# Batches 2 and 3 of the attention in plain fp32 on halves of the array, and the second layer's weights decoded beside it

## The chip, the core and the metric

The kernel runs on one core of a Trainium2 chip. The metric is the device time of one execution in microseconds (us). The engines are TensorE (PE, with its weight loads as PEld), VectorE (DVE), ScalarE (ACT) and GpSimd (POOL); SyncE (SP) issues nearly all of the DMAs. SBUF is the on-chip memory, PSUM the eight banks that TensorE writes.

## The reference

Attention over 4 batches, 8 heads, 576 positions and 64 columns, with a retrieved memory mixed in, and behind it two matrix products with a gated activation between them, all in fp32:

```python
scores = scale * q @ k.T          # causal mask, softmax -> a
local = a @ v
q_p = where(q > 0, q, exp(q) - 1) + 1
mem_out = (q_p @ M_prev) / (q_p . z_prev + 1e-6)
x = g * mem_out + (1 - g) * local  # g = sigmoid(beta), one per head; x is 2304 x 512
h = x @ w_in                       # w_in 512 x 2048, given as 8-byte floats
out = (h * sigmoid(1.702 * h)) @ w_out   # w_out 2048 x 512, given as 8-byte floats
```

## The kernel before

**Stages.** The work is planned in slots. `first_queries` (0 to 46 us) does the first 256 queries of batch 0 and decodes the first of the sixteen blocks of `w_in`. Then sixteen pairs of heads (four batches, four pairs each) run through `plan_prep` and `plan_attend`: pair p starts at slot `K0[p]`, batch 0 at slots 0, 7, 14, 21, the others 8 slots apart from 29 on, so batch 1 has slots 29 to 61 and batches 2 and 3 slots 61 to 133. `step()` emits what is planned for a slot, and then fills TensorE with matmuls of the first layer (`first_moe`) up to a budget per slot (`PACE`, 2.2 us at first, 2.7 us from slot 60). It charges each matmul a modelled time (`mm`). The first layer takes 8 chunks of tokens (256 to 320 wide) times 16 blocks times 12 matmuls, 1536 in all. After the last pair, a tail emits the rest of them (390 to 463 us). Then the second layer runs (463 to 653 us), a product of 2 by 2 blocks in seven partial products: `units` of 12 matmuls each, 84 units.

**Attention, two ways.** `plain = b < MP` with `MP = 2`: batches 0 and 1 multiply in plain fp32 with both heads side by side on halves of the array (`s_both`: 64 rows for each head; `pv_both`: 64 columns for each head). Their matmuls are issued in unbroken groups (`group`), which wait once for all that they need. Batches 2 and 3 multiply in fp32r: operands are split into a high part and a rest. `split_hi` (ACT), `split_lo_k`, `split_lo_q`, `vlo` (POOL) split keys, queries and values; `stack_hi` and `stack_lo` copy them by DMA into the tiles `W0` and `W1`; `s_unit` and `pv_unit` multiply; `ev_unit` splits each piece of the transposed weights (ACT copy, DVE subtraction); `xsum` adds the two halves of the result. One fp32 matmul stands in the trace as two records.

**The first layer's results.** `gate` copies each block from PSUM into a tile `hk` (three buffers), on ACT or, for every second block, on DVE while `len(moe_ps) == 1`, which is until the tail; then SP stores it to DRAM (`gd`, line 856). Blocks go to the two banks `ps_m`; in the tail, from the 21st block on (`LATE = 20`), to the six banks `ps_w`.

**The second layer's weights.** `conv_pair(kk)` runs in the tail for kk = 0 to 7, two in five steps. For both halves it loads 512 KB of raw `w_out` on POOL's queue (line 983), scales it into a bank of `ps_w` (`scale`, ACT, line 987), and puts the bits together (`bits`, three DVE instructions, lines 992, 993, 995). Then `sums` makes the four sums that the seven products need (DVE), `w_hi` copies them to fp32r (ACT), and `w_lo` subtracts (DVE), giving the tile `wo{kk}`. For kk = 0 to 4 (`EARLY`) that is done in the tail, for 5 to 7 behind it. The unit n needs the tiles 2p and 2p+1, where p = n mod 4.

**The seam.** `split(n)` makes the operands of unit n (`oh` on ACT, `ol` on DVE) from a tile of `gd` that `load_g` (line 1030) brought back and `gelu` (ACT, line 1034) passed through. The first two units' operands are loaded early. The other tiles of the second layer lie over the first layer's: in the list of pools behind `left.close()`, `reuse_waits="tile"` makes each wait only for the tiles that lay under it.

Tile schedules the program: the order on each engine and queue comes from priorities and a timeline that it keeps, not from the text alone.

The lines of the helpers: `mm` 126, `tr` 132, `copy` 137 (ACT) and 140 (DVE), `tt` 145. The max of the softmax is line 546, the exponentials 552, the scaling of rows 555, the second layer's matmul 1071.

Of the kernel before, what the change touches and what calls it, by code (L numbers as in the profile page):

```python
# [8 lines left out]
F32 = mybir.dt.float32  # L9
# [25 lines left out]
def tile_attention_memory_moe(ctx, tc, kq, vq, mem, zz, beta, w_in, w_out, out):  # L35
# [4 lines left out]
    MP = 2  # L40
# [3 lines left out]
    LATE = 20  # L44
    W0 = 6
    CONV = [-7, -6, -5, -3, -1, 1, 3, 5, 7, 9]
    PSUM = bass.MemoryType.PSUM
# [13 lines left out]
    dr = pool(ctx, "dr", space=bass.MemoryType.DRAM)  # L61
    ldp = pool(attn, "ldp", side="right")
# [335 lines left out]

    def load_vq(p):
        b, c = pairs[p]  # L400

        vr = (att.tile([128, 5, 128], F32, name="vs", bufs=2) if b < MP else ldp.tile([128, 5, 128], F32, name="vr"))
# [10 lines left out]
    def plan_prep(p):  # L413
# [3 lines left out]
        rest, plain = b < MB, b < MP  # L417
        T0 = 2 if rest else 0
        qo = 256 if rest else 0

        def split_hi():
            kqr = raws[p]["kq"]
            P["hi"] = att.tile([128, S + SQ], F32R, name="hi")
            copy("A", P["hi"][:, :S + SQ - qo], kqr[:, :S + SQ - qo])

        def split_lo_k():
            P["lok"] = att.tile([128, S], F32R, name="lok")
            sub("P", P["lok"], raws[p]["kq"][:, :S], P["hi"][:, :S])

        def split_lo_q():  # L430
            P["loq"] = att.tile([128, SQ], F32R, name="loq")
            n = SQ - qo
            sub("P", P["loq"][:, :n], raws[p]["kq"][:, S:S + n], P["hi"][:, S:S + n])

        def stack_hi():
            P["W"] = [att.tile([128, S + 1024 - 2 * qo], F32R, name=f"W{h}", bufs=2) for h in range(2)]
            for h in range(2):
                r, o = slice(64 * h, 64 * h + 64), slice(64 - 64 * h, 128 - 64 * h)
                w = f32(P["W"][h])
                n = S + 512 - qo  # L440
                nc.sync.dma_start(w[r, :n], f32(P["hi"])[r, :n])
                nc.sync.dma_start(w[o, S:n], f32(P["hi"])[r, S:n])

        def stack_lo():
            for h in range(2):
                r, o = slice(64 * h, 64 * h + 64), slice(64 - 64 * h, 128 - 64 * h)
                nc.sync.dma_start(f32(P["W"][h])[o, :S], f32(P["lok"])[r, :])
                n = 512 - qo
                for rows in (r, o):
                    nc.sync.dma_start(f32(P["W"][h])[rows, S + n:S + 2 * n], f32(P["loq"])[r, :n])  # L450

        def vhi():
            P["vs"] = att.tile([128, 5, 2, 2, D], F32R, name="vs", bufs=2)
            copy("A", P["vs"][:, :, :, 0], raws[p]["v"].rearrange("p t (h d) -> p t h d", h=2))

        def vlo():
            sub("P", P["vs"][:, :, :, 1], raws[p]["v"].rearrange("p t (h d) -> p t h d", h=2),
                P["vs"][:, :, :, 0])
# [4 lines left out]

        def msplit():
            P["ms"] = att.tile([128, 2, 2, D], F32R, name="ms", bufs=2)
            copy("A", P["ms"][:, :, 0], raws[p]["m"], gt[:, c:c + 1])
            nc.vector.scalar_tensor_tensor(
                out=P["ms"][:, :, 1], in0=raws[p]["m"], scalar=gt[:, c:c + 1], in1=f32(P["ms"][:, :, 0]),
                op0=ALU.mult, op1=ALU.subtract)
# [38 lines left out]
        def qev():  # L508
            qh, ql = P["qpt"] = [att.tile([128, S], F32R, name=f"qpt{s}", bufs=2) for s in range(2)]
            if plain:  # L510
                P["qpt"] = att.tile([128, S], F32, name="qpt0", bufs=2)
                used(P["pt"][0], copy("A", P["qpt"][:, qo:512], P["pt"][0][:, qo:]))
                used(P["pt"][1], copy("V", P["qpt"][:, 512:S], P["pt"][1][:, :64]))
                return
            for pt, a, n in ((P["pt"][0][:, qo:], qo, 512 - qo), (P["pt"][1], 512, 64)):
                copy("A", qh[:, a:a + n], pt[:, :n])
                sub("V", ql[:, a:a + n], pt[:, :n], qh[:, a:a + n])
# [7 lines left out]
        if plain:  # L525
            at(s0 + 7, 51, mplain)
        else:
            at(s0 + 6, 55, vhi)
            at(s0 + 7, 50, vlo)
            at(s0 + 7, 51, msplit)  # L530
# [26 lines left out]
    def plan_attend(p):  # L557
# [4 lines left out]
        rest, plain = b < MB, b < MP  # L562
# [18 lines left out]

        def s_unit(h, i):
            n, q0 = 128 * (i + 1), S + 128 * i - qo
            q1 = q0 + 512 - qo
            ps = U["ps", h, i] = bank("ps")
            mm(ps[:, :n], P["W"][h][:, q0:q0 + 128], P["W"][h][:, :n], True, False)
            mm(ps[:, :n], P["W"][h][:, q1:q1 + 128], P["W"][h][:, :n], False, True)
# [30 lines left out]
        def s_tail():  # L618
            U["ps"] = [bank("ps") for _ in range(2)]
            o = 512 - qo  # L620
            if plain:
                kq = raws[p]["kq"]
                for f in range(2):
                    mm(U["ps"][f][:, :CH], kq[:, S + o:S + o + 128], kq[:, CH * f:CH * f + CH], True, True)
                return
            hi, lok, loq = P["hi"], P["lok"], P["loq"]
            qh, ql = hi[:, S + o:S + o + 128], loq[:, o:o + 128]
            for k, (st, mv) in enumerate(((qh, hi), (qh, lok), (ql, hi))):
                for f in range(2):
                    mm(U["ps"][f][:, :CH], st, mv[:, CH * f:CH * f + CH], k == 0, k == 2)  # L630
# [38 lines left out]
        def ev_unit(h, j):  # L669
            n = 384 if j < 0 else (320 if j < 3 else 256)  # L670
            pt = U["pt", h, j]
            if plain:
                U["e", h, j] = att.tile([128, 384], F32, name=f"e{(j + h) % 2}", bufs=4)
                x = copy("AV"[(j + h) % 2], U["e", h, j][:, :n], pt[:, :n])
                used(pt, x)
                U["ev", h, j] = x.ins.name
                return
            e = U["e", h, j] = [att.tile([128, 384], F32R, name=f"e{s}", bufs=4) for s in range(2)]
            copy("A", e[0][:, :n], pt[:, :n])
            sub("V", e[1][:, :n], pt[:, :n], e[0][:, :n])  # L680

        def pv_unit(h, j):
            ch = 0 if j < 0 else 1
            q0, n = (0, 256) if ch == 0 else (256, 320)
            first, last = j <= 0, j < 0 or j == 3
            if first:
                U["po", h, ch] = ps_o.tile([128, 512], F32, name="po")
            po, e, vs = U["po", h, ch], U["e", h, j], P.get("vs")
            ops = []

            def put(o, kt, x, y):
                for s in range(2):
                    ops.append((o, vs[:, kt, h].rearrange("p s d -> p (s d)"), e[s][:, x:y]))

            if first:
                for s in range(2):
                    ops.append((po[:, :n], P["ms"][:, h].rearrange("p s d -> p (s d)"), P["qpt"][s][:, q0:q0 + n]))
            if j < 0:
                put(po[:, :256], 0, 0, 256)
                put(po[:, 128:256], 1, 256, 384)  # L700
            elif j < 3:
                put(po[:, :320], j, 0, 320)
            else:
                put(po[:, :192], 3, 0, 192)
                put(po[:, 128:192], 4, 192, 256)
            for k, (o, l, r) in enumerate(ops):
                mm(o, l, r, first and k == 0, last and k == len(ops) - 1)
# [27 lines left out]

        def xsum(h, ch):
            r, o = slice(64 * h, 64 * h + 64), slice(64 - 64 * h, 128 - 64 * h)
            q0, n = (0, 256) if ch == 0 else (256, 320)
            if "xf" not in P:
                P["xf"] = wkp.tile([128, S], F32, name="xf")  # L740
# [58 lines left out]
        if plain:  # L799
            steps = ((3, 1), (2, 5)) if rest else ((3, 1), (2, 4), (1, 5), (0, 5))  # L800
            for i, idx in steps:
                if i:
                    at(k0 + idx, 20, lambda i=i: scores((1, 0) if i == 1 else (i,)))
# [404 lines left out]
```

## Time and profile before

| | us |
|---|---|
| median of 3 runs (650.18, 654.70, 655.16) | 654.7 |
| the profiled execution | 654.82 |
| its span, first to last instruction | 653.0 |
| around the span | 1.8 |

The span falls into the start (0 to 38 us), batch 0 (to 109 us), batch 1 (to 188 us), batches 2 and 3 (to 390 us), the tail of the first layer (to 463 us), the seam (to 480 us) and the second layer (to 653 us). The mean granted clock of TensorE is 0.988 of full speed. Matmuls are pipelined: a record's length is longer than the distance to the next one, so a cost is read from start to start. A line of the trace can be that of a helper, so groups are told apart by tiles: `ps` are scores, `pt` transposes, `po` weighted values, `pm` the first layer, `acc` the second.

### The profile page before, as it was taken

The page shows a single profiled execution, that of the slowest core. Times are in us where ns is not written, and L with a number is a line of the kernel's source. Part 1 is how long each engine was busy: PE and PEld are TensorE (multiplying, and loading weights), DVE is VectorE, ACT ScalarE, POOL GpSimd, SP SyncE. Part 2 cuts the span into 40 slices and gives each one's busy share as a digit, 9 for nine tenths or more (in the row PEclk, how much of TensorE's full clock was granted, in tenths as well). Part 3 has the DMA queues.
Part 4 walks back from the last instruction along what each step waited for, and adds up shares of the span by engine and source line. Part 5 has one row for each costly group of instructions (what it writes and reads, how often), then busy time and mean ns, then how long its engine had stood idle before and what let it go on. Part 6 is the DMA issues. An engine that isn't in the chain of part 4 may idle for free.

```text
span 653.0 us, 12028 instructions
## 1 busy us (share of the span) xinstructions
PE 600.2 (92%) x4016; PEld 547.7 (84%) x4016; DVE 454.0 (70%) x1097; ACT 399.7 (61%) x919; POOL 218.1 (33%) x276
## 2 busy tenths in 40 slices
PE   3779799999988999998999997899799999999996
PEld 2548665688757899998999997899699999999996
DVE  4889776645676577757577635986897579559943
ACT  4767556535575777668576545565886764775451
POOL 3647545533469666457574320310000000000000
PEclk9989999999999999999999999999989999999999
DMA  7948753314529866785671136765835640771002
GB/s 244 314 134 258 214 162 131 108 50 157 158 78 226 222 186 169 213 218 167 198 201 66 47 112 231 231 195 185 263 131 159 177 148 1 217 210 57 26 0 74
DMA packets 65647, 103.47 MB, mean 158 GB/s; under 512 B 6960, under 2 KB 49456, under 8 KB 65584
## 3 DMA queue, kind: packets, MB, share of 16 engines
q1 hardware_dynamic: 63280, 94.30, 48.1%
q0 software_dynamic: 2304, 8.39, 4.2%
q8 instruction: 32, 0.52, 0.4%
q14 instruction: 31, 0.25, 0.1%
HBM read 62.87 MB, written 26.69 MB: 137 GB/s over the span
## 4 chain that ended last, share of the span: by engine, by line
PE 65%; DMA 14%; DVE 8%; ACT 7%; issue 4%; SPq 1%; POOL 1%; DVEq 0%; ACTq 0%; POOLq 0%
PE acc L1071 26%; PE pm L126 18%; PE po L126 7%; PE pt L132 6%; PE ps L126 6%; DMA gd<-hk 5%; DMA xl<-xd 4%; DMA xd<-xf 2%; ACT a L552 2%; DVE ps L546 1%; DMA g<-gd 1%; DMA fq<-in_vq_dram 1%; ACT oh L137 1%; ACT hk L137 1%; ACT xh L137 1%
## 5 line engine op out<-in xcount | busy, mean ns | idle before, releaser
L126 PE MATMUL pm<-xh,wi 128*128 128x288 f32 (+2 forms) x1024 | 217.6, 302 | 14.2 <-ACT hk L137 8.1
L126 PEld LDWEIGHTS pm<-xh,wi 128*128 128x128 f32 x1024 | 165.9, 190 | 19.6 <-ACT hk L137 10.1
L1071 PE MATMUL acc<-oh,wo 128*128 128x384 f32 x672 | 160.1, 340 | 4.7 <-ACT oh L137 4.5
L126 PE MATMUL pm<-xl,wi 128*128 128x288 f32 (+2 forms) x512 | 152.0, 299 | 0.2 <-DVE xl L145 0.2
L1071 PEld LDWEIGHTS acc<-oh,wo 128*128 128x128 f32 x672 | 121.5, 190 | 6.6 <-ACT oh L137 6.3
L145 DVE TENSOR_TENSOR ol<-g,oh 128x768 fp32r<-128x768 f32 x84 | 79.3, 954 | 49.8 <-ACT oh L137 48.5
L1071 PE MATMUL acc<-ol,wo 128*128 128x384 f32 x336 | 99.4, 338 | 0.0
L126 PEld LDWEIGHTS pm<-xl,wi 128*128 128x128 f32 x512 | 96.6, 189 | 1.7 <-DVE sm L612 1.1
L137 ACT ACTIVATE oh<-g 128x768 fp32r<-128x768 f32 x84 | 70.5, 841 | 44.2 <-PE acc L1071 43.8
L555 POOL TENSOR_SCALAR a<-a,sm,g 128x512 f32<-128x512 f32 (+3 forms) x112 | 71.7, 651 | 73.0 <-DVE sm L612 60.3
L552 ACT ACTIVATE a<-ps,nm 128x512 f32<-128x512 f32 (+3 forms) x112 | 60.2, 542 | 47.0 <-DVE nm L546 46.0
L546 DVE CUSTOM_DVE_ANT_0 ps<-ps,mask 128x256 f32<-128x256 f32 (+4 forms) x144 | 68.5, 499 | 26.9 <-PE ps L126 22.8
L1071 PEld LDWEIGHTS acc<-ol,wo 128*128 128x128 f32 x336 | 62.6, 189 | 0.0
L137 ACT ACTIVATE e<-pt 128x320 fp32r<-128x320 f32 (+4 forms) x116 | 47.4, 436 | 22.6 <-PE pt L132 12.0
L126 PE MATMUL po<-e,vs 128*64 128x320 f32 (+6 forms) x416 | 58.2, 321 | 2.9 <-ACT e L137 2.9
L137 ACT ACTIVATE hk<-pm 128x288 f32<-128x288 f32 (+2 forms) x84 | 33.5, 406 | 40.8 <-DMA gd<-hk 19.1
L126 PEld LDWEIGHTS po<-e,vs 128*128 128x128 f32 (+1 forms) x416 | 46.6, 165 | 13.1 <-ACT e L137 3.6
L132 PE MATMUL pt<-ident,a 128*128 128x128 f32 x296 | 54.9, 273 | 0.0
L145 DVE TENSOR_TENSOR e<-pt,e 128x320 fp32r<-128x320 f32 (+1 forms) x80 | 37.2, 485 | 25.2 <-ACT e L137 24.0
L1034 ACT ACTIVATE g<-g 128x768 f32<-128x768 f32 x48 | 40.2, 842 | 13.8 <-DMA g<-gd 12.5
L145 DVE TENSOR_TENSOR g<-g,g 128x768 f32<-128x768 f32 x48 | 44.1, 950 | 0.2
L132 PE MATMUL pt<-ident,at 128*128 128x128 f32 x160 | 41.1, 281 | 3.4 <-ACT a L552 2.3
(144 smaller groups left out, 916.8 us busy)
## 6 DMA issues: line engine op xcount, KB each, us to landing
g<-gd SPq DMA_DIRECT2D x48, 384.0 KB, 3.8
gd<-hk SPq DMA_DIRECT2D x96, 144.0 KB, 3.1
wraw<-in_w_in_dram SPq DMA_DIRECT2D x16, 512.0 KB, 4.8
wraw<-in_w_out_dram POOLq DMA_DIRECT2D x16, 512.0 KB, 4.5
kqr<-in_kq_dram SPq DMA_DIRECT2D x8, 608.0 KB, 5.2
W<-hi SPq DMA_DIRECT2D x16, 272.0 KB, 4.0
W<-loq SPq DMA_DIRECT2D x32, 128.0 KB, 3.7
qr<-in_vq_dram SPq DMA_DIRECT2D x12, 320.0 KB, 3.1
```

The lines of the kernel that those rows point to most:

```text
L126: x = nc.tensor.matmul(out, l, r, start=start, stop=stop)
L132: nc.tensor.transpose(out, in_, idn)
L137: return nc.scalar.activation(out=dst, in_=src, func=AF.Copy, **kw)
L145: (nc.vector if eng == "V" else nc.gpsimd).tensor_tensor(out=dst, in0=a, in1=b, op=op)
L546: nc.vector.tensor_tensor_reduce(out=ps, in0=ps, in1=mk, op0=ALU.add, op1=ALU.min, scale=-0.125, scalar=1e38 if j == 0 else nm[:, j - 1:j] ...
L552: return nc.scalar.activation(out=a, in_=ps, func=AF.Exp, scale=-1.0, bias=nm, accum_out=sm)
L555: (nc.vector if eng == "V" else nc.gpsimd).tensor_scalar(out=a, in0=a, scalar1=r, scalar2=gcol, op0=ALU.mult, op1=ALU.mult)
L1034: nc.scalar.activation(out=t, in_=t, func=AF.Gelu_apprx_sigmoid)
L1071: nc.tensor.matmul(acc[b, j][:, :QN], W[2 * p + kk][:, WPART[i], sp, 128 * j:128 * j + 128], mv[:, kk], start=first and p + kk == 0 and sp ...
```

## The change

- `plain` is gone: every batch takes the path of batches 0 and 1. With it go the splits of keys, queries and values, the tiles `hi`, `lok`, `loq`, `W0`, `W1` and the DMAs that fill them, the splits in `ev_unit` and `qev`, and `xsum`. Keys and values of all batches have two buffers (`kqf`, `vr`).
- `decode(i)` for i = 0 to 15 loads half a pair of `w_out` on SP's queue and, two slots later, scales and decodes it in place in SBUF. The slots are 27, 29, ... 41 and 62, 65, ... 83. The decoded tiles stay in two new pools of four buffers of 4 KB, `rr` (left side, behind the first layer's weights) and `rl` (right side).
- `conv_pair` keeps `sums`, `w_hi` and `w_lo` alone, for kk = 0 to 3 (`EARLY = 4`), once in six steps; `sums` of these writes into the room of the raw weights. For kk = 4 to 7 all three run behind the tail.
- `gate` copies every second block on DVE in the tail too.
- `LATE = 4`: from the 5th block of the tail on, blocks take the six banks.
- The raw blocks 7, 9, ... 15 of `w_in` are loaded into `rr` instead of the tag `W1`. The second layer's saved sums share `rl`. Behind `left.close()` there are four tiles `w2` in two places of the list.

```diff
-    MP = 2
-    LATE = 20
+    LATE = 4
+    DECODE = [27 + 2 * i for i in range(8)] + [62 + 3 * i for i in range(8)]
+    EARLY = 4
+    rl = pool(ctx, "rl", 4, side="right")
...
-        if b < MP:
-            kqr = att.tile([128, S + SQ], F32, name="kqf", tag="W0", bufs=2)
-        else:
-            kqr = ldp.tile([128, S + SQ], F32, name="kqr")
+        kqr = att.tile([128, S + SQ], F32, name="kqf", bufs=2)
...
-        if not plain:
-            at(s0 + 1, 50, split_hi)
-            at(s0 + 3, 50, split_lo_k)
-            at(s0 + 3, 51, split_lo_q)
-            at(s0 + 3, 52, stack_hi)
-            at(s0 + 4, 52, stack_lo)
...
-            copy("AV"[blk % 2 == 0 and len(moe_ps) == 1], h[:, :w], ps[:, :w])
+            copy("AV"[blk % 2 == 0], h[:, :w], ps[:, :w])
...
-        raw = (att, {"tag": "W1", "bufs": 2}) if other else (cnv, {"bufs": 2})
+        raw = (rr, {"tag": "r"}) if other else (cnv, {"bufs": 2})
...
+    rr = pool(left, "rr", 4, side="left")
...
+    def decode(i):
+        kk, h = divmod(i, 2)
+        if h == 0:
+            raw2[kk] = (rr if kk < EARLY else rl).tile([128, 2, DM], F32, name="r", tag="r")
+        raw = cnv.tile([128, DM, 2], I32, name="wraw", bufs=2)
+        r = raw2[kk][:, h]
+        ri = r.bitcast(I32)
+
+        def scale():
+            nc.scalar.activation(out=r, in_=raw[:, :, 1].bitcast(F32), func=AF.Copy, scale=2.0 ** -112)
+
+        def bits():
+            nc.vector.tensor_scalar(out=ri, in0=ri, scalar1=3, scalar2=None, op0=ALU.logical_shift_left)
+            nc.vector.scalar_tensor_tensor(
+                out=ri, in0=raw[:, :, 1], scalar=-2 ** 31, in1=ri, op0=ALU.bitwise_and, op1=ALU.bitwise_or)
+            nc.vector.scalar_tensor_tensor(
+                out=ri, in0=raw[:, :, 0], scalar=29, in1=ri, op0=ALU.logical_shift_right, op1=ALU.bitwise_or)
+
+        nc.sync.dma_start(raw.rearrange("p f w -> p (f w)"), w_out[kk + KK * h].bitcast(I32))
+        at(state["slot"] + 2, 56, scale)
+        at(state["slot"] + 2, 57, bits)
+
+    for i, slot in enumerate(DECODE):
+        at(slot, 58, lambda i=i: decode(i))
...
+    def sums(kk):
+        if kk < EARLY:
+            st = cnv.tile([128, 4, DH], F32, name="st", tag="wraw", bufs=2)
+        else:
+            st = stg.tile([128, 4, DH], F32, name="st")
...
     def conv_pair(kk):
-        box = {}
         s0 = state["slot"] + 1
...
+        at(s0, 60, lambda: sums(kk))
+        at(s0 + 1, 40, lambda: new_w(w2a, kk))
+        at(s0 + 1, 41, lambda: w_hi(kk))
+        at(s0 + 1, 42, lambda: w_lo(kk))
...
-    conv_q = list(range(KK))
+    conv_q = list(range(EARLY))
...
-        if (k % 5 in (2, 4) or fill["gen"] is None) and conv_q:
+        if (k % 6 == 3 or fill["gen"] is None) and conv_q:
...
-    w2b = [pool(ctx, f"w2_{kk}", side="left", reuse_waits="tile") for kk in range(EARLY, KK)]
+    w2b = [pool(ctx, f"w2_{kk}", side="left", reuse_waits="tile") for kk in (4, 5)]
     pools[1, 1] = pool(ctx, "g11b", 2, side="left", reuse_waits="tile")
     pools["op", 1] = pool(ctx, "opb", side="left", reuse_waits="tile")
+    w2b += [pool(ctx, f"w2_{kk}", side="left", reuse_waits="tile") for kk in (6, 7)]
     pools[0, 0] = pool(ctx, "g00", 4, side="left", reuse_waits="tile")
     for kk in range(EARLY, KK):
+        sums(kk)
         new_w(w2b[kk - EARLY], kk)
         w_hi(kk)
         w_lo(kk)
```

## Rows read from the trace of the kernel before

**Rows 1.** The page: busy time of each engine, share of the span, instructions.

```profile
PE 600.2 (92%) x4016; PEld 547.7 (84%) x4016; DVE 454.0 (70%) x1097; ACT 399.7 (61%) x919; POOL 218.1 (33%) x276
```

**Rows 2.** Busy us (instructions) by stretch: PE, PEld, DVE, ACT, POOL; then clock, DMA.

```profile
109.30:148.00 38.70, 36.51 (x250) 27.39 (x248) 22.28 (x80) 19.09 (x55) 17.23 (x20) 1.00 0.30 98
148.00:172.40 24.40, 24.40 (x178) 20.48 (x176) 12.83 (x46) 10.84 (x33) 8.41 (x11) 1.00 0.37 123
172.40:206.50 34.10, 30.46 (x217) 21.71 (x216) 22.98 (x87) 23.63 (x73) 24.81 (x30) 1.00 0.64 167
206.50:390.00 183.50, 178.19 (x1367) 174.75 (x1366) 123.54 (x396) 122.28 (x343) 99.58 (x114) 1.00 0.58 164
390.00:463.40 73.40, 65.82 (x490) 64.20 (x489) 55.81 (x100) 43.69 (x88) 9.85 (x16) 1.00 0.65 207
```

**Rows 3.** The chain that ended last, in order of time: start, us, what.

```profile
425.65 16.08 PE pm L126 x120
```

**Rows 4.** Who waited for whom, 390 to 463.4 us: total, times, longest.

```profile
ACT hk L137 <- DMA gd<-hk: 13.8, 8, 4.3
PE pm L126 <- ACT hk L137: 7.6, 7, 1.7
```

**Rows 5.** Timeline of PE, a pair of batch 1 (plain): start, us, what.

```profile
163.55 0.31 PE L126 MATMUL pm<-xl,wi 128*128 128x320 f32 x1
163.70 0.46 PE L126 MATMUL pm<-xh,wi 128*128 128x320 f32 x2
164.09 0.92 PE L126 MATMUL ps<-kqf 64*128 64x384 f32 x4
164.93 0.76 PE L126 MATMUL po<-qpt,ms 128*64 128x320 f32 x4
165.52 2.23 PE L126 MATMUL po<-e,vs 128*64 128x320 f32 x20
167.68 0.77 PE L132 MATMUL pt<-ident,qp 128*128 128x128 f32 x5
```

**Rows 6.** Timeline of PE, pairs of batches 2 and 3 (split).

```profile
242.23 0.54 PE L126 MATMUL ps<-W 128*128 128x384 f32 x2
242.60 0.42 PE L126 MATMUL pm<-xh,wi 128*128 128x288 f32 x2
...
385.79 0.45 PE L126 MATMUL po<-qpt,ms 128*128 128x320 f32 x2
386.08 1.41 PE L126 MATMUL po<-e,vs 128*128 128x320 f32 x10
```

**Rows 7.** Groups by form: busy us, mean ns; idle before, releaser.

```profile
L992 DVE TENSOR_SCALAR ws<-ws 128x512 int32<-128x512 int32 x16 | 10.9, 691 | 5.7 <-ACT ws L987 5.7
L993 DVE SCALAR_TENSOR_TENSOR ws<-wraw,ws 128x512 int32<-128x512 int32 x16 | 10.9, 687 | 0.1
L995 DVE SCALAR_TENSOR_TENSOR r<-wraw,ws 128x512 int32<-128x512 int32 x16 | 10.7, 679 | 0.1
L987 ACT ACTIVATE ws<-wraw 128x512 f32<-128x512 f32 x16 | 9.8, 627 | 0.3 <-DVE r L995 0.3
L145 POOL TENSOR_TENSOR loq<-kqr,hi 128x640 fp32r<-128x640 f32 x8 | 12.5, 1561 | 0.0
L145 DVE TENSOR_TENSOR wo<-st,wo 128x1024 fp32r<-128x1024 f32 x8 | 9.8, 1219 | 1.9 <-ACT wo L137 1.9
```

**Rows 8.** The seam: timeline of PE [idle before <- who ended it].

```profile
467.63 0.34 PE L1071 MATMUL acc<-ol,wo 128*128 128x384 f32 x1
472.43 1.65 PE L1071 MATMUL acc<-oh,wo 128*128 128x384 f32 x4 [4.46 <-ACT oh L137]
```

**Rows 9.** The seam by stretch, columns as in rows 2.

```profile
472.00:474.00 2.00, 1.57 (x5) 1.58 (x6) 1.08 (x2) 2.00 (x4) 0.00 (x0) 0.50 0.99 339
474.00:476.00 2.00, 2.00 (x8) 2.00 (x7) 1.90 (x3) 1.42 (x2) 0.00 (x0) 0.50 0.93 268
```

**Rows 10.** Tile `ms` on DVE, two SBUF inputs: ns min/median/max, first and last start.

```profile
L467 DVE SCALAR_TENSOR_TENSOR ms<-mr,gt,ms x8: 351/626/1182, 188.0 to 356.7; 128x128 fp32r<-128x128 f32 x8
```

More of the change, by code (lines that the diff above doesn't have):

```diff
@@ L416, in plan_prep @@
         P = prep[p] = {}
-        rest, plain = b < MB, b < MP
+        rest = b < MB
         T0 = 2 if rest else 0
         qo = 256 if rest else 0
[L421 to L458, printed above, removed]
         def mplain():
@@ L561, in plan_attend @@
         U = {}
-        rest, plain = b < MB, b < MP
+        rest = b < MB
         qo = 256 if rest else 0
@@ L619, in s_tail @@
             U["ps"] = [bank("ps") for _ in range(2)]
[L620 to L630, printed above, removed]
+            o, kq = S + 512 - qo, raws[p]["kq"]
+            for f in range(2):
+                mm(U["ps"][f][:, :CH], kq[:, o:o + 128], kq[:, CH * f:CH * f + CH], True, True)
         def max_tail():
@@ L671, in ev_unit @@
             pt = U["pt", h, j]
[L672 to L707, printed above, removed]
+            U["e", h, j] = att.tile([128, 384], F32, name=f"e{(j + h) % 2}", bufs=4)
+            x = copy("AV"[(j + h) % 2], U["e", h, j][:, :n], pt[:, :n])
+            used(pt, x)
+            U["ev", h, j] = x.ins.name
         def pv_both(j):
@@ L797, in flush @@
                 group(*late)
[L799 to L803, printed above, removed]
-        for i, idx in (steps if plain else ((3, 1), (2, 3), (1, 5), (0, 7))):
+        for i, idx in ((3, 1), (2, 5)) if rest else ((3, 1), (2, 4), (1, 5), (0, 5)):
+            if i:
+                at(k0 + idx, 20, lambda i=i: scores((1, 0) if i == 1 else (i,)))
+            k = k0 + idx
             for h in range(2):
-                k = k0 + idx + (h if i and not plain else 0)
-                if not plain:
-                    at(k, 10, lambda h=h, i=i: s_unit(h, i))
                 at(k + 1, 10, lambda h=h, i=i: max_unit(h, i))
@@ L813, in plan_attend @@
                 at(k + 2 + (h if i >= 2 else 0), 10, lambda h=h, i=i: scale_unit(h, i))
-        order = [(h, j) for h in range(2) for j in range(4)]
-        if plain:
-            order = [(h, j) for j in range(4) for h in range(2)]
+        order = [(h, j) for j in range(4) for h in range(2)]
         if not rest:
@@ L940, in tile_attention_memory_moe @@
     moe_ps.append((ps_w, "pm2"))
-    KK = NB // 2
-    EARLY = 5
     QN = 384
@@ L972, in conv_pair @@
     def conv_pair(kk):
-        box = {}
         s0 = state["slot"] + 1
-        def room():
-            raw2[kk] = [stg.tile([128, DM], F32, name=f"r{h}") for h in range(2)]
-            raw2[kk].append(stg.tile([128, 4, DH], F32, name="st"))
-        at(s0 + 2, 59, room)
-        def load(h):
-            box["raw", h] = (cnv, stg)[kk % 2].tile([128, DM, 2], I32, name="wraw", bufs=2)
-            nc.gpsimd.dma_start(box["raw", h].rearrange("p f w -> p (f w)"), w_out[kk + KK * h].bitcast(I32))
@@ L999, in sums @@
-        def sums():
-            ra, rb, st = raw2[kk]
-            tt("V", st[:, 0], ra[:, DH:], rb[:, DH:], ALU.add)
-            tt("V", st[:, 1], st[:, 0], ra[:, :DH], ALU.subtract)
-            tt("V", st[:, 2], ra[:, :DH], ra[:, DH:], ALU.subtract)
-            tt("V", st[:, 3], rb[:, :DH], st[:, 1], ALU.subtract)
-        for h in range(2):
-            at(s0, 5, lambda h=h: load(h))
-            at(s0 + 2, 60, lambda h=h: scale(h))
-            at(s0 + 2, 61, lambda h=h: bits(h))
-        at(s0 + 3, 60, sums)
```

84 lines of the change are left out of this document (20 added, 64 removed).

## The prediction

> **What bounds the kernel now.** I read the page first, then the busy time by stretch, then who waited in the tail, then single pairs and the seam on TensorE's timeline.
>
> TensorE is busy for 92% of the span [rows 1]. By stretch, length less busy time is what it sat idle: 2.2 us in 109 to 148, nothing in 148 to 172, 3.6 in 172 to 206, 5.3 in 206 to 390, 7.6 in the tail [rows 2]. So TensorE bounds every stage, and a change that doesn't shorten its own work can win only those idle pieces and the seam. The reader is to see that the share of the other engines (DVE 70%, POOL 33%) matters only where it makes TensorE wait.
>
> The 7.6 us of the tail have one cause. TensorE waits seven times for the copy of `hk` on ACT, 7.6 us in all, and these copies wait eight times, 13.8 us in all and 4.3 at the longest, for the store of an earlier `hk` [rows 4]: three buffers, two banks, and a DMA system at 0.65 of its time [rows 2] because sixteen raw blocks of `w_out` come in at the same time.
>
> At the seam TensorE runs two units without a pause, ends at 467.97 and starts again at 472.43, 4.46 us later, released by an `oh` on ACT [rows 8]. Behind the pause the granted clock is 0.50, the lower of its two levels (1.2 GHz), for at least 3.57 us of busy time [rows 9]; at half speed that loses 1.8. The seam costs 6.3 us.
>
> **The change, part by part**, against the profiled execution: 653.0 us of span and 1.8 around it, 654.8; the median of the runs, 654.7, is the same.
>
> 1. Plain instead of split on TensorE. Read from start to start: the larger part of the weighted values took 164.93 to 167.68, 2.75 us for both heads, in plain fp32 [rows 5], and 385.79 to 387.49, 1.70 us for one head, 3.40 for both, split [rows 6]. Plain wins 0.65. A block of scores of 384 columns took 0.84 for both heads in plain [rows 5] and 0.37 a head, 0.74, split [rows 6]. Plain loses 0.1 a block, 0.4 for four blocks. Entering a group costs too: the two `pm` before the scores take 0.39 together, where one takes 0.15 [rows 5], so 0.09 is lost; with some five changes a pair, 0.45. The sum is +0.2 a pair, **+1.6** for the eight pairs. Bounds: only the values' gain, -5.2; only the losses, +6.8.
>
> 2. The planner's charge. From the formula in `mm`, one pair is charged 7.8 us plain against 7.2 split, so about 35 first-layer matmuls of 0.134 us [rows 3] leave the attention for the tail: 4.7 us less there, 4.7 more here. Zero in the sum.
>
> 3. The work that goes from the other engines in batches 2 and 3. A pair gives up three subtractions on POOL of the kind of `loq` at 1.56 us [rows 7], a split and a subtraction for each of ten transposed pieces, and all the DMAs into `W0` and `W1`; in 172 to 206 POOL was busy 24.8 of 34.1 us [rows 2]. What can come back is the 8.9 us for which TensorE sat idle in 172 to 390 [rows 2]. A part of it is the first layer waiting for batch 1's result to go through DRAM, which stays. I take less than half, **-4**; bounds 0 and -8.9. New waits: the values' two buffers are freed only by the previous pair's last product, and on SP's queue the next loads and the stores of `hk` stand behind that load. Batch 1 already runs so, and TensorE sat idle for nothing in 148 to 172 [rows 2], so this costs nothing; without that cover the stores would be late and TensorE would wait for `hk` as in the tail.
>
> 4. Decoding beside the attention. A half pair costs DVE 0.691 + 0.687 + 0.679 = 2.06 us and ACT 0.63 [rows 7], sixteen times. Eight of them belong to slots 29 to 43, that is to 109 to 148 us. DVE is busy 22.3 of 38.7 us there [rows 2]; with 8 x 2.06 = 16.5 it has 38.8. That is all of it. But the decode has low priority, no one waits for it before the tail, and behind it lie 11.6 free us of DVE (24.4 less 12.8) [rows 2], so it can slide. Each instruction still stands for up to 0.7 us in front of a maximum of the softmax that TensorE needs. I take **+2**; bounds 0 and +16.5, all eight on the path. The other eight lie in batch 2, where DVE gives up more than they bring: 0. ACT has room everywhere (19.1 of 38.7). The loads move from POOL's queue to SP's; a load waits for its raw buffer, which the decode before the last one frees, and stores of `hk` and the next pair's keys stand behind it. That is late only if DVE is, so it is in this term.
>
> The Trainium skill, VectorE: DVE Perf Modes, section on the perf-mode tiers, has `tensor_scalar` on fp32 at twice the rate where all operands lie in SBUF, which the new place of the shift allows; no row here shows a shift there, and by the rule a decode would take some 0.3 us less, my estimate, 2.7 less in the stretch.
>
> 5. The tail. Of the waits in [rows 4], the loads go (the DMA system has the stores alone), ACT gives up half of the copies and sixteen scalings of 0.63 us [rows 7], DVE gives up 33 us of bits (16 x 2.06) and takes half of the copies, and six banks hold six blocks of 12 x 0.134 = 1.6 us [rows 3], 9.6 us, from the fifth block on: more than the longest lateness of a store, 4.3 us. I take **-6.5** of 7.6; bounds -2 and -7.6.
>
> 6. The seam. Four tiles instead of three are now converted behind the tail. By the sizes of the tiles the last one, `wo7`, lies 256 bytes over the weights of block 15, the last of the first layer, so its copies can't start before TensorE has ended there (T). Three copies on ACT of up to 1024 columns and the last subtraction of 1.22 us [rows 7] make it ready at about T+3.4. The operands of unit 2 lie over the `st` of that conversion, so they come at about T+4.4. The two units before last from 463.4 to 467.97, 4.6 us [rows 2, 8]. It just fits; every other instruction that ACT or DVE puts in between shows. Before, DVE came to the seam with a backlog (55.8 of 73.4 us [rows 2]), now without one. I take about half, **-3.5**; bounds -6.3 and +4 (a pause twice as long).
>
> 7. The raw blocks of `w_in` in `rr`: by the sizes, `rr` starts 320 bytes inside the room of the first queries, so block 7 may load some us later, while the other odd blocks have four buffers instead of two. 0, within 1 either way. The second layer's sums in `rl`: the same depth, 0.
>
> Sum: 654.8 + 1.6 - 4 + 2 - 6.5 - 3.5 = **644.4**, rounded to 644.
>
> **The rivals.**
>
> A. The tail alone gains. For it: idle TensorE time in 172 to 390 is made of waits for the data's way through DRAM, and the seam is now bound by `wo7`. Against it: POOL's 24.8 of 34.1 us [rows 2]. 654.8 + 1.6 + 2 - 6.5 = 652.
>
> B. DVE becomes the bound in batch 1, and the kernel gets slower. Place: slots 29 to 45. DVE has 38.8 us of work for 38.7 (point 4). What would add to it: the decode's second and third instruction now read two SBUF operands, where before one lay in PSUM. The one kind of such an instruction on DVE that runs beside POOL's work took 0.351 us at the least and 1.182 at the most [rows 10], so 0.83 is what another engine can cost it; sixteen such, at POOL's share of 17.2 in 38.7 us [rows 2], make 16 x 0.83 x 0.45 = 6. All decodes on the path and this: +22.5 instead of +2, 665; without the lock 659. It decides from 12.4 us on, where it eats the other gains. Against it: nothing needs the decode early. The Trainium skill, SBUF — State Buffer, section on practical consequences, says that a DVE instruction with two SBUF inputs contends with a GpSimd instruction that reads SBUF, and that one blocks fully; the spread of [rows 10] agrees.
>
> C. All idle pieces go. 654.8 + 1.6 - 8.9 - 7.6 - 6.3 = 634. For it: every wait named has lost its cause; against it: DRAM's way in 172 to 212 stays.
>
> **How the numbers follow.** My forecast (638 to 650) has 0.52, A 0.25, B 0.12, C 0.11. About 1% (6.5 us) is what a measurement of this kernel can tell from no change. Faster by more: most of the first and all of C, 0.57. Within 1%: A, the rest of the first, the milder half of B, 0.33. Slower by more: the rest of B, 0.10. The range goes from C to the near end of B: 633 to 657, which leaves out 2 in 10.
>
> **What would show it.** In the profile after: no wait of `pm` for `hk` of over 2 us in the tail (point 5); plain pairs of batches 2 and 3 with TensorE busy as in 148 to 172 (points 1, 3); a pause of TensorE at the seam of at most 3 us, and the granted clock staying at 1.00 there (point 6); decoding on DVE in the gaps between 109 and 188 us, with that stretch at most 3 us longer (point 4). The prediction is wrong if batch 1 grows by over 5 us, if waits for `wo` take the place of the pause at the seam, or if stores of `hk` wait on SP's queue behind a load of raw weights.

## The result, and the profile after

The changed kernel takes 661.7 us (median of 4 runs, 660.2 to 661.9); the kernel before, beside it, 653.4 (650.2 to 655.2). The ratio is 1.0128, with a 95% interval of 1.0081 to 1.0175: slower by 1.3%, where 644 was forecast. The profiled execution has a span of 660.1 us, against 653.0.

The page's busy row of after, which answers [rows 1]:

```profile
PE 606.1 (92%) x4000; PEld 523.6 (79%) x4000; DVE 424.7 (64%) x1036; ACT 352.8 (53%) x811; POOL 182.9 (28%) x237
```

VectorE, ScalarE and GpSimd gave up work, and TensorE has as many instructions as before (4000 and 4016), though they keep it busy 5.9 us longer. So the loss is not a longer list of work but a worse place for it. By stretch, columns as in [rows 2]; the cuts are the starts of the first pair, of batch 1, of its third and fourth pair, of the second pair of batch 2 and of the last pair, and the end of the first layer:

```profile
37.80:115.10 77.30, 66.15 (x412) 48.33 (x410) 66.99 (x172) 47.62 (x117) 40.84 (x38) 0.94 0.66 212
115.10:164.70 49.60, 42.94 (x270) 32.72 (x268) 43.84 (x125) 24.33 (x65) 21.51 (x22) 0.93 0.49 161
164.70:187.90 23.20, 23.20 (x170) 19.29 (x168) 11.64 (x40) 10.54 (x33) 7.50 (x11) 1.00 0.35 113
187.90:225.10 37.20, 30.05 (x203) 19.60 (x201) 21.03 (x84) 20.57 (x64) 19.10 (x25) 0.95 0.35 110
225.10:368.20 143.10, 138.58 (x1046) 115.11 (x1044) 74.16 (x260) 70.22 (x214) 59.60 (x77) 1.00 0.41 124
368.20:471.90 103.70, 103.70 (x797) 98.01 (x796) 49.65 (x121) 43.92 (x104) 17.82 (x22) 1.00 0.35 113
```

The second row is the piece that took 38.7 us before [rows 2]: 49.6 now, with DVE busy for 43.8 of it (22.3 before) and TensorE idle for 6.7 (2.2). The last row is a tail in which TensorE never stops. From the start of the first pair to that of batch 2, before and after:

```profile
38.10:188.00 149.90, 138.52 (x938) 103.98 (x936) 102.22 (x316) 82.32 (x229) 73.52 (x83) 0.98 0.47 144
37.80:203.60 165.80, 145.21 (x937) 108.53 (x935) 133.03 (x377) 92.32 (x244) 77.67 (x80) 0.95 0.54 172
```

With one instruction fewer, TensorE is idle 9.2 us more and busy 6.7 us longer. The granted clock has a part in that: 5% of 165.8 us is 8.3 us of full speed that was not granted, 2% of 149.9 is 3.0. Up to 5 of the 15.9 us are the clock's, and they are in the prices below too.

The new instructions on DVE, by form (ns min/median/max, first and last start), which answer [rows 7]:

```profile
L818 DVE TENSOR_SCALAR r<-r x16: 412/426/867, 73.6 to 146.9; 128x512 int32<-128x512 int32 x16
L819 DVE SCALAR_TENSOR_TENSOR r<-wraw,r x16: 622/682/1630, 75.5 to 148.5; 128x512 int32<-128x512 int32 x16
L821 DVE SCALAR_TENSOR_TENSOR r<-wraw,r x16: 670/681/1102, 79.4 to 150.6; 128x512 int32<-128x512 int32 x16
```

That is the surprise: all sixteen decodes ran between 73.6 and 151 us, none in batches 2 and 3. A slot says when a step is written out; nothing holds its instructions there. The loads went out from 68 to 142 us, eight of the sixteen in the moment in which a raw buffer came free; SP's waits for that, 60 to 165 us (total, times, longest):

```profile
SPq L824 <- DVE r L821: 23.0, 8, 5.0
```

From the chain that ended last, in order of time:

```profile
89.38 4.46 DMA wraw<-in_w_out_dram
93.86 0.67 ACT r L815
94.53 0.68 ACT a L488 x2
...
124.56 0.69 DVE ps L482
125.32 0.55 DVE r L819
125.86 0.33 DVE st L147
126.20 0.61 DVE ps L482
126.86 0.55 DVE r L821
127.41 0.62 DVE e L142 x2
128.06 0.42 DVE r L818
```

Read the second piece as a queue: a maximum of the softmax (`ps L482`), a piece of a decode, a sum of the second layer (`st`), a maximum, a piece of a decode, a copy of `e`. In this stretch the chain runs through DVE and no longer through TensorE: of the 52 us from 84 to 136, DVE has 32.3, the DMAs 9.4 and TensorE 2.6, where before DVE had 4.6 and TensorE 36.0. The sums slid forward as well. Sixteen of the 32, those of the four `conv_pair`, were written out for the tail and ran at 118 to 153 us, at 0.42 us each 6.7 us of DVE more; all kernels below whose decode lies early have them early too.

To compare kernels whose order differs, I cut every trace at the start of the first pair, of batch 2 and of the last pair, and at the end of the first layer, and take from each part 0.134 us [rows 3] for every record of the tile `pm` that started in it (the first layer's matmuls, and in the first part of every kernel the same eight of `first_queries`, so that no difference changes by them); what is left is attention and waiting ("net"). For before: 149.9 - 383 x 0.134 = 98.6, 162.4 - 528 x 0.134 = 91.7, 113.2 - 624 x 0.134 = 29.6, and 184.2 for the second layer.

```
                                net b0,1  net b2,3  net tail  2nd layer   median  ratio to before
before                            98.6      91.7      29.6      184.2     653-655
after                            114.4      95.5      18.4      183.7     661.7   1.0128
plain alone                       95.6      98.3      22.3      183.2     647.3   0.9891
plain, hk alternating             94.8      94.9      29.1      182.5     650.7   0.9981
after, no bits                   110.0      97.0      18.4      184.2     660.7   1.0114
after, slots held                100.7     103.2      19.7      184.3     658.3   1.0064
  slots 69..129                   95.7     101.0      18.5      183.8     648.4   0.9913
  slots 69..129, hk on ACT        94.0     103.3      19.6      183.3     649.0   0.9941
  slots 69..129, LATE = 20        94.1      99.8      20.0      183.2     649.1   0.9915
  slots 67..127                   96.7     106.5      19.0      183.6     655.8   1.0029
  eight of them at the end        93.4      99.8      20.0      184.4     649.5   0.9950
  slots 10..40 (control)         111.7      94.9      18.4      184.0     661.2   1.0142
  control, no bits               100.3      97.9      18.4      184.2     651.4   0.9987
  control, no loads              113.6      96.4      18.4      185.3     659.7   1.0112
```

Kernels with the same instructions up to a point differ there by up to 3.5 us from trace to trace (rows "slots 69..129" and the two under it; "plain alone" and the row under it), so a smaller difference between two single traces says nothing. From before to after the columns give +15.8, +3.8, -11.2 and -0.5: batches 0 and 1 lose more than the tail wins.

### The profile page after: what moved, and what is told of

The parts are those of the page before. It is cut to its first block, busy times and chain, and to the rows that moved or that the text cites. A ratio compares the mean times of both kernels' runs of the same rounds, so it can differ in the third digit from the quotient of the medians.

```text
span 660.1 us, 11489 instructions
## 1 busy us (share of the span) xinstructions
PE 606.1 (92%) x4000; PEld 523.6 (79%) x4000; DVE 424.7 (64%) x1036; ACT 352.8 (53%) x811; POOL 182.9 (28%) x237
## 4 chain that ended last, share of the span: by engine, by line
PE 62%; DMA 14%; DVE 12%; ACT 6%; issue 3%; POOL 1%; SPq 1%; DVEq 0%; ACTq 0%; POOLq 0%
PE pm L128 27%; PE acc L942 15%; PE pt L134 7%; PE po L128 6%; PE ps L128 6%; DMA g<-gd 4%; DMA wraw<-in_w_in_dram 3%; DVE g L147 2%; DMA wraw<-in_w_out_dram 2%; DMA xd<-xf 2%; DVE ol L147 2%; DMA xl<-xd 1%; DVE ps L482 1%; ACT a L488 1%; ACT oh L139 1%
## 5 line engine op out<-in xcount | busy, mean ns | idle before, releaser
L128 PE MATMUL pm<-xl,wi 128*128 128x288 f32 (+2 forms) x512 | 154.6, 304 | 1.1 <-DVE xl L147 1.0
L491 POOL TENSOR_SCALAR a<-a,sm,g 128x512 f32<-128x512 f32 (+3 forms) x112 | 75.7, 687 | 114.0 <-DVE sm L541 93.0
L482 DVE CUSTOM_DVE_ANT_0 ps<-ps,mask 128x256 f32<-128x256 f32 (+4 forms) x144 | 67.7, 504 | 54.4 <-PE ps L128 52.0
L128 PEld LDWEIGHTS pm<-xl,wi 128*128 128x128 f32 x512 | 98.4, 193 | 2.5 <-DVE xl L147 1.6
L488 ACT ACTIVATE a<-ps,nm 128x256 f32<-128x256 f32 (+2 forms) x112 | 59.8, 541 | 55.4 <-DVE nm L482 54.7
L128 PE MATMUL ps<-kqf 128*128 128x288 f32 (+4 forms) x288 | 69.5, 482 | 4.7 <-ACT at L488 1.6
L142 DVE COPY hk<-pm 128x288 f32<-128x288 f32 (+2 forms) x64 | 29.1, 454 | 47.0 <-PE pm L128 40.5
L139 ACT ACTIVATE hk<-pm 128x288 f32<-128x288 f32 (+2 forms) x64 | 26.2, 411 | 58.7 <-PE pm L128 53.1
L128 PEld LDWEIGHTS po<-e,vr 128*64 128x64 f32 x416 | 29.9, 137 | 20.1
L128 PEld LDWEIGHTS ps<-kqf 64*128 64x128 f32 (+1 forms) x288 | 30.6, 190 | 18.8 <-issue 8.6
```

The costliest lines, as they stand in the source:

```text
L128: x = nc.tensor.matmul(out, l, r, start=start, stop=stop)
L139: return nc.scalar.activation(out=dst, in_=src, func=AF.Copy, **kw)
L142: return nc.vector.tensor_copy(dst, src)
L482: nc.vector.tensor_tensor_reduce(out=ps, in0=ps, in1=mk, op0=ALU.add, op1=ALU.min, scale=-0.125, scalar=1e38 if j == 0 else nm[:, j - 1:j] ...
L488: return nc.scalar.activation(out=a, in_=ps, func=AF.Exp, scale=-1.0, bias=nm, accum_out=sm)
L491: (nc.vector if eng == "V" else nc.gpsimd).tensor_scalar(out=a, in0=a, scalar1=r, scalar2=gcol, op0=ALU.mult, op1=ALU.mult)
```

## The experiments

The theories: **T1**, the bits on DVE, pulled forward, keep TensorE waiting for the softmax. **R2**, it is the sixteen loads of `w_out`, in SP's queue and in the DMA system. **R3**, plain attention itself costs in batches 2 and 3.

**No bits.** One line out:

```
-        at(state["slot"] + 2, 57, bits)
```

> The changed kernel with the three DVE instructions that assemble the bits of a decoded half pair left out (16 x 3 instructions, some 33 us of DVE); the loads of w_out, the scalings on ACT and all else stay. It leaves out the bit assembly, so its second layer runs on other numbers than the reference's. Theory T1 (the decode was pulled forward to 72 to 151 us, fills DVE there, and TensorE waits for the maxima and copies of the softmax): batch 1 goes back to its old length, the pair that starts at 187.9 us starts at 172 to 175, and the time is 644 to 649. Rival R2 (the loads of w_out on SP's queue are what is late, or the rate of DMA): no change, 658 to 662. Rival R3 (plain attention in batches 2 and 3 is what costs): at most the tail's share comes back, 656 to 662.

Measured: 660.7, ratio 1.0114 (1.0056 to 1.0173), as R2 and R3 had it. T1 as I had put it falls: without the bits the loss is still there. The chain shows what took their place:

```profile
79.60 5.63 DMA wraw<-in_w_out_dram
85.25 0.68 ACT r L815
85.94 5.14 DMA wraw<-in_w_out_dram
91.11 0.69 ACT r L815
...
97.19 5.10 DMA qr<-in_vq_dram
```

A raw buffer comes free as soon as ACT has scaled it, so the loads follow each other without a break, and the next pair's queries stand behind them: `qr` took 5.10 us to land, where 3.1 is the median of such loads before. By stretch, columns as in [rows 2]:

```profile
82.00:98.00 16.00, 12.88 (x87) 8.26 (x85) 8.37 (x29) 10.85 (x28) 5.83 (x8) 1.00 0.85 282
98.00:110.00 12.00, 10.38 (x45) 6.43 (x42) 9.14 (x27) 8.01 (x20) 3.22 (x4) 0.74 0.84 289
```

The DMA system is at 0.85, and the granted clock falls to 0.74 behind TensorE's pauses. So the run changed two things, the bits and the spacing of the loads, and can't tell T1 from R2. The three kernels "slots 10..40" below hold the spacing still.

**Slots held, and held late.** Each load waits for the matmul written out last before its slot, so nothing can run ahead of it:

```
         x = nc.tensor.matmul(...)
+        state["last"] = x.ins.name
...
-        nc.sync.dma_start(raw..., w_out[kk + KK * h]...)
+        ld = nc.sync.dma_start(raw..., w_out[kk + KK * h]...)
+        tc.add_manual_dep(ld.ins, state["last"], SYNC, reason="slot")
...
-    DECODE = [27 + 2 * i for i in range(8)] + [62 + 3 * i for i in range(8)]
+    DECODE = [69 + 4 * i for i in range(16)]          # the late one only
```

> The changed kernel with one wait more for each load of w_out: it waits for the last matmul that was written out before the slot to which the list DECODE gives it, so that no decode can run earlier than its slot. The slots stay: eight from 29 to 43, eight from 64 to 85. T1: eight decodes move out of batch 1 into batch 2, where DVE has room: half of what batch 1 lost comes back, the pair at 187.9 starts at 178 to 183, the time is 650 to 656. R2: the loads are as many and SP's queue now stands still for them, 658 to 665. R3: 658 to 662.

> As the run before, with the same waits, but the sixteen slots are 69, 73, ... 129, all in batches 2 and 3, so that no decode lies in batch 1. T1: batch 1 as in the kernel before (the pair at 187.9 starts at 171 to 174), the gain in the tail kept, 643 to 649. R2: 656 to 664. R3: 656 to 662. Were T1 right of batch 1 but DVE not free in batches 2 and 3 either, the stretch from 225 to 368 us (11.9 us a pair) would grow and the time be 650 to 656.

Measured: 658.3 (ratio 1.0064, 1.0028 to 1.0100) with the slots of the change, 648.4 (0.9913, 0.9877 to 0.9950) with the late ones. The late ones came out as T1 says (643 to 649): batch 1 as before, the tail's gain kept. The first did not: T1 had 650 to 656, and 658.3 lies in the ranges of R2 and R3. It is the important one for the prediction: it is the kernel I had costed, eight decodes in batch 1 and eight in batch 2, and it is slower than before all the same. Its net in batches 0 and 1 is 5.8 above the mean of the seven other kernels without an early decode (94.9; before's own 98.6, not in it, has some 3 us more than they in the first two pairs of batch 0), and in batches 2 and 3 it is 6.8 above the mean of the seven plain kernels that decode elsewhere (96.4): 0.7 and 0.85 us for each decode.

**Plain alone.** The kernel before with

```
-    MP = 2
+    MP = 4
```

> The kernel before with plain fp32 attention in all four batches (MP = 4) and nothing else: decode, tail and seam as before. By points 1 to 3 of the prediction 654.8 + 1.6 - 4 = 652 (bounds 646 to 661). T1 (plain attention is not at fault): 649 to 655. R3 (it is): 657 to 664, with the pairs from 206 us on longer than in the kernel before.

Measured: 647.3, ratio 0.9891 (0.9814 to 0.9967), below all that was expected. R3 falls as an explanation of the loss, but my account of the gain falls too: batches 2 and 3 are not shorter (98.3 net, 91.7 before); what is shorter is the tail, which this edit hardly touches. Who waited in the tail, 390 to 458 us:

```profile
PE pm L126 <- ACT hk L137: 2.7, 3, 1.5
...
ACT hk L137 <- DMA gd<-hk: 5.0, 5, 1.5
```

Both waits of [rows 4] are a third of what they were (7.6 and 13.8). The loads of `w_out` end at 438 us here and at 450 before, but that does not settle it: with alternating copies (below) they end at 436, and TensorE waits for `hk` 7.0 us all the same. Why this one tail is short stays open.

**The decode early, taken apart.** A control with the slots where the changed kernel had run by itself, and the control without the bits, and without the loads (the bits then work on a tile that lies in SBUF anyway):

```
+    DECODE = [10 + 2 * i for i in range(16)]
...
-        at(state["slot"] + 2, 57, bits)                                     # no bits
...
-        raw = cnv.tile([128, DM, 2], I32, name="wraw", bufs=2)              # no loads
+        raw = wb[0].bitcast(I32).rearrange(...)
...
+            tc.add_manual_dep(x.ins, last, SYNC, reason="slot")             # on the scaling
...
-        nc.sync.dma_start(raw..., w_out[kk + KK * h]...)
```

> Control for the next two: the changed kernel with each load of w_out held by a wait on a matmul of its slot, slots 10, 12, ... 40, which is about where the changed kernel ran its decodes by itself (loads from 68 to 142 us). All theories: about as the changed kernel, 655 to 664, the pair that starts batch 2 at 184 to 190 us (188 in the kernel before it was, 203.6 in the changed kernel), so 196 to 206 here.

> The control without the three DVE instructions that assemble the bits (loads and scalings stay; it leaves out the bit assembly). The run without bits before it had lost as much as the changed kernel, but there the loads had also bunched up. T1 (DVE work alone costs): 644 to 649. R2 (the loads, in SP's queue and in the DMA system, cost): within 3 us of the control. Both together, each with its half: 4 to 10 us under the control.

> The control without the sixteen loads of w_out: scaling and bits work on a tile of first-layer weights that lies in SBUF, and the scaling carries the wait of its slot (it leaves out w_out, so its second layer computes on other numbers). T1: within 3 us of the control, 653 to 664. R2: 643 to 650, batch 2 starts at 187 to 191 us. Both: 4 to 10 us under the control.

Measured: 661.2, 651.4 and 659.7 (ratios 1.0142, 0.9987, 1.0112; intervals 1.0078 to 1.0206, 0.9948 to 1.0025, 1.0036 to 1.0188). The control answers for the changed kernel; without the bits 10 us come back, without the loads nothing that counts. Most of the decode's stretch, from the last pair of batch 0 to the third of batch 1, in the three, columns as in [rows 2]; control, no bits, no loads:

```profile
95.40:163.00 67.60, 56.97 (x352) 41.22 (x348) 60.15 (x161) 35.61 (x92) 28.58 (x26) 0.92 0.57 183
```

```profile
95.10:150.10 55.00, 49.96 (x319) 36.11 (x317) 35.35 (x119) 34.55 (x91) 24.02 (x27) 0.97 0.62 203
```

```profile
101.40:165.90 64.50, 57.73 (x341) 40.63 (x339) 54.45 (x151) 34.04 (x90) 26.84 (x28) 0.89 0.26 79
```

DVE is busy for 60 of 67.6, 35 of 55 and 54 of 64.5 us; the DMA share is 0.57, 0.62 and 0.26. The time goes with the first, not with the second. T1 holds for most of the loss, once the loads are spaced; by what was expected, the run without bits (9.9 under the control) is the far end of "both", and the run without loads (1.6 under it) is T1's. Without the bits some 5 us of net stay above the mean without decodes (100.3 and 94.9). What is still early there is the loads, the scalings on ACT and the sixteen sums (116 to 144 us); these were not told apart.

**The tail's parts.** Plain alone with the copies of `hk` alternating; and, on the kernel with slots 69 to 129, the copies on ACT alone and LATE = 20:

```
-            copy("AV"[blk % 2 == 0 and len(moe_ps) == 1], h[:, :w], ps[:, :w])
+            copy("AV"[blk % 2 == 0], h[:, :w], ps[:, :w])
...
-    LATE = 4
+    LATE = 20
```

> The kernel before with plain attention in all batches (as in the run with that alone, 647.3) and one thing more: the copies of hk in the tail alternate between ACT and DVE. Decode stays in the tail. If the copies on ACT alone were what TensorE waited for there: the 2.7 us of waits of pm for hk go, 643 to 646. If the stores of hk, slowed by the loads of w_out, were: 646 to 649.

> The changed kernel with its sixteen decodes held in slots 69 to 129 (that run took 648.4) and the copies of hk in the tail on ACT alone again, as in the kernel before; ACT has no scalings there now. If the alternation is what shortened the tail: waits of pm for hk come back, the tail is 3 to 7 us longer, 651 to 655. If it was the loads and the decode that left: no change, 646 to 650.

> As the run with slots 69 to 129, with LATE = 20 again, so that the tail's first twenty blocks go through two banks instead of the first four. If the banks shortened the tail: 650 to 654. If not: 646 to 650.

Measured: 650.7 (0.9945 to 1.0017), 649.0 (0.9899 to 0.9982) and 649.1 (0.9879 to 0.9951). The first is above both expectations, the other two are where no change was expected. While the decode is in the tail, the alternation doesn't help: TensorE still waits for `hk` on both engines (the kernel with plain attention and alternating copies, 390 to 460 us):

```profile
PE pm L126 <- ACT hk L137: 5.8, 6, 2.9
PE pm L126 <- DVE hk L140: 1.2, 1, 1.2
```

Once the decode has left, neither the alternation nor the banks matter (net tail 18.5, 19.6, 20.0). So taking out the decode and its loads is enough to shorten it; which of the two does it was not tried. With both still in the tail its net was 29.6, 29.1 and, in plain alone, 22.3.

**The place within a pair.** The same sixteen decodes, held two slots earlier, and eight of them moved to the end:

```
-    DECODE = [69 + 4 * i for i in range(16)]
+    DECODE = [67 + 4 * i for i in range(16)]
...
+    DECODE = [69 + 6 * i for i in range(8)] + [115 + 2 * i for i in range(8)]
```

> As the run with slots 69 to 129, with every decode two slots earlier (67 to 127), so that the bits fall on slots 0 and 4 of a pair instead of 2 and 6, where the maxima of the softmax are. If it is the place within a pair that made these pairs 1 to 3 us longer than without a decode (six pairs, some 7 us): 643 to 646. If it is DVE's time as such: 647 to 650.

> As the run with slots 69 to 129, with eight decodes at 69, 75, ... 111 and eight at 115, 117, ... 129, in the last pair and the start of the tail, where TensorE has first-layer matmuls beside it. If a decode costs only where TensorE waits for the softmax: attention loses half as much, 643 to 647. If the eight at the end delay the copies of hk: 649 to 654.

Measured: 655.8 (ratio 1.0029, 0.9994 to 1.0063) and 649.5 (0.9950, 0.9913 to 0.9987). The first went against both of my expectations: two slots cost 7.4 us, in the other direction than I had thought. DVE had the same work in both (batches 2 and 3, columns as in [rows 2]; slots 69 to 129, then 67 to 127):

```profile
185.00:358.40 173.40, 162.04 (x1180) 129.75 (x1178) 105.96 (x342) 87.52 (x260) 71.70 (x92) 0.99 0.49 155
```

```profile
186.60:363.90 177.30, 161.30 (x1167) 127.73 (x1165) 106.76 (x347) 87.76 (x260) 71.79 (x92) 0.99 0.46 151
```

What differs is where it stands. From the chain of the slower one:

```profile
311.40 0.37 SPq L403
...
311.82 6.86 DMA wraw<-in_w_out_dram
318.70 0.68 ACT r L816
...
320.22 0.60 DVE r L820
...
321.07 0.69 DVE r L822
321.76 0.60 DVE r L820
322.36 0.34 DVE st L148
322.70 0.61 DVE ps L483
```

SP had waited with the load of a pair's values (L403), the raw loads stood behind it, and two decodes then came in a row, in front of a maximum (`ps L483`). It is so all along: the slower one's sixteen scalings start two by two, 1.3 to 2.4 us apart, where the faster one's lie 9.4 to 16.1 us apart up to 357 us. So the edit moved the place within a pair and the spacing, and the run doesn't tell these apart. Eight at the end did not win more than the even spacing.

## Why the prediction was wrong

**Point 4, the decode, was mis-sized, and this decided it.** It put +2 on sixteen decodes (bounds 0 and +16.5), all of it in batch 1 and nothing on the eight in batch 2; the net of batches 0 and 1 grew by 15.8. Its own sign of being wrong came: batch 1 went from 78.7 to 88.5 us. Two things failed in it. First, "eight belong to slots 29 to 43": that took a slot for a time, and said that the decode could slide later, when it slid earlier, all sixteen at once. By the medians this is the smaller part: with the slots held, 658.3 against 661.7, and there the eight in batch 2 that were put at 0 cost 6.8 us. Second, the sum compared DVE's busy time with the length of the stretch and took what was free as cover. There is no such cover: in a pair each maximum, copy and scaling has one right moment, and TensorE waits for it, with little else to do in the last pair of batch 0 and the first of batch 1 (6 first-layer matmuls in each); these two grew by 7.3 us net, the pairs before and behind them by 5.5 and 3.8. The price of one decode, 1.8 us on DVE by the medians, came out by its place, with the sums and the clock in it: 1.0 to 1.2 us at 68 to 151 us, 0.7 to 0.85 with the change's slots held, 0.6 two by two at slots 67 to 127, 0.3 singly at 69 to 129. Point 4's sentence on 0.7 us in front of a maximum named the mechanism; sixteen times three such instructions should have been priced by it.

**Rival B is what happened** in its kind: DVE became the bound in that stretch and the kernel slower. That its time was met as well (659 to 665, measured 661.7) is luck: it put eight decodes in full, 2.06 us each, on the path of batch 1, and sixteen came at about 1 us each, from batch 0 on, while the tail won more than was put in. The argument against it, that nothing needs the decode early, is true and doesn't help: what is ready is taken. Its lock between DVE and POOL was there: of the 32 two-input instructions of the decode in after, the 15 with no POOL instruction beside them took 0.67 to 0.69 us, and the 17 others 0.83 in the mean and 1.63 at most. That sums to some 2.5 us, not to 6. The Trainium skill, SBUF — State Buffer, section on practical consequences, has a DVE instruction with two SBUF inputs contend with a GpSimd instruction that reads SBUF; the trace agrees. And the lock is not what sets the price: with slots 67 to 127 all 32 took 0.68 to 0.69, and that was the dearest of the late places; with 69 to 129, half as dear, twelve stood beside POOL and took 0.94 in the mean. The second instruction with slots 67 to 127, as above:

```profile
L820 DVE SCALAR_TENSOR_TENSOR r<-wraw,r x16: 679/686/693, 219.4 to 396.1; 128x512 int32<-128x512 int32 x16
```

**Point 1 came to nothing where TensorE is full, and one of its readings was wrong.** After, a pair of batch 3, timeline of TensorE, which answers [rows 5, 6]:

```profile
336.90 0.92 PE L128 MATMUL ps<-kqf 64*128 64x384 f32 x4
337.75 0.76 PE L128 MATMUL po<-qpt,ms 128*64 128x320 f32 x4
...
340.49 0.76 PE L134 MATMUL pt<-ident,qp 128*128 128x128 f32 x5
```

The scores take 0.85 and the values 2.74 (0.84 and 2.75 were put in). But the split values' 1.70 was read to the end of their last record, since TensorE pauses behind it. Another pair of before has a matmul right behind the same twelve:

```profile
313.31 0.45 PE L126 MATMUL po<-qpt,ms 128*128 128x320 f32 x2
...
314.84 0.44 PE L132 MATMUL pt<-ident,at 128*128 128x128 f32 x2
```

That is 1.53 a head, 3.06 for both: plain wins 0.31 a pair and not 0.65, and by its own terms point 1 comes to +4.3 and not +1.6. The runs show neither: the five pairs from the third of batch 2 to the third of batch 3 take 62.2 us net before and 61.9 after.

**Point 3 had the wrong sign.** Points 1 and 3 together put -2.4 on batches 2 and 3; they cost +3.8 net, and in the seven plain kernels that decode elsewhere 94.9 to 98.3 against 91.7. POOL and the DMA system were relieved as said (POOL 102.8 to 70.9 us between the start of batch 2 and the last pair), but no one had waited for them. The +4 lies in the first two pairs of batch 2, 42.3 us before and 46.4 after, with 96 first-layer matmuls in both: the stretch that waits for batch 1's result to go through DRAM, which the point itself said would stay. There TensorE waits 2.5 us for `xh`, which is made of that result, where it waited 1.0, and the granted clock is 0.96 where it was 1.00, up to 1.9 us of 46.4. Why that wait is longer with plain attention was not tried.

**Point 2** changed nothing, as said, and moved 12 matmuls, not 35. **Point 5 was right and too small**: -11.2 net where -6.5 was put; no wait of `pm` for `hk` is left after 390 us, and the stores keep ACT and DVE waiting for 3.5 and 3.3 us, where it was 13.8. Of its reasons only the first, loads and decode gone, was needed. The waits of [rows 4] were 7.6 us; for the other 3.6 the trace shows no cause.

**Point 6 went as a pause and not as time.** The seam, timeline of TensorE, which answers [rows 8], and who waited from there to the end:

```profile
475.68 0.34 PE L942 MATMUL acc<-ol,wo 128*128 128x384 f32 x1
477.76 0.96 PE L942 MATMUL acc<-oh,wo 128*128 128x384 f32 x4 [1.74 <-ACT oh L139]
```

```profile
PE acc L942 <- DVE ol L147: 2.3, 4, 1.1
PE acc L942 <- ACT oh L139: 2.1, 2, 1.7
```

The pause is 1.74 instead of 4.46 and the granted clock stays at 1.00, but four waits for `ol` take its place; the waits sum to 4.4 where one of 4.5 stood, and from the first layer's end to TensorE's last instruction it is 183.7 after 184.2: -0.5 where -3.5 was put. The seam itself did win: 48 matmuls into the layer the changed kernel is 4.7 us ahead, with no half clock behind the pause. After 104 it is 2.3 ahead, at the end 0.4. The lead goes into waits for operands: those above and, from 500 us on, those of the weight loads (1.5 us in all in the same stretch before):

```profile
PEld acc L942 <- ACT oh L139: 2.2, 5, 0.6
PEld acc L942 <- DVE ol L147: 1.3, 3, 0.6
```

The point had left out that what it won could be waited away later in the layer. **Point 7** was right: with no decode early, batches 0 and 1 take 93.4 to 96.7 net with `rr`, and 94.8, 95.6 and (before) 98.6 without.

The sum as it came: +15.8 + 3.8 - 11.2 - 0.5 - 0.3 (an earlier start of the first pair) = +7.6, where the spans say +7.1. The range missed because it ended at the near end of rival B, whose chance of 0.12 was too small.

The two best versions beat both kernels by about as much: plain attention alone (647.3) and the whole change with its decodes held at slots 69 to 129 (648.4). What the tail wins by losing the decode, the decode costs again in batches 2 and 3.

## What to carry to other kernels

Free time of an engine in a stretch isn't cover: price an inserted instruction by what stands behind it on its queue, and by whether TensorE has other work in that moment. A step written out late, with low priority and no true dependence, can run as early as its buffers allow; if it must not, make its load wait for something, and try more than one place. When an experiment takes away an instruction, look whether it also set the pace of something else.

## What the runs showed of the hardware

The shift by three takes 0.426 us with both operands in SBUF, where it took 0.691 on PSUM [rows 7]; the Trainium skill, VectorE: DVE Perf Modes, section on the perf-mode tiers, has fp32 at twice the rate from SBUF, and the trace agrees in direction, at a factor of 1.6 for this int32 shift of 512 elements. Beside POOL the same shift rose to 0.867, though it has only one tensor as input.
